# Linear attention with a gated output: units of 256 tokens in a hand-ordered order of two steps, instead of chunks of 128 tokens over all batches

## The chip, the cores and the metric

The kernel runs on one NeuronCore of a Trainium2 chip. The metric is the device time of one execution in microseconds, as the median of three runs. The engines are TensorE (PE, matmuls; PEld is its weight loading), VectorE (DVE), ScalarE (ACT), GpSimd (POOL), and SyncE (SP), which here only issues DMAs. [...] TensorE writes to PSUM[...]. All other tiles lie in SBUF.

## The reference

Batch 4, 8 heads of 48, 768 tokens; r, k, v are float32. First comes a recurrence for every batch and head, with a decay w per channel and a bonus u for the token itself:

```
for t in range(S):
    y[t]  = r[t] @ (state + (u*k[t]) outer v[t])
    state = w[:, None] * state + k[t] outer v[t]
```

The heads side by side give x, 384 wide, and a gated layer follows:

```
gate_pre[t] = sum over j < 5 of conv_w[j] * x[t - 4 + j]      # causal, per channel
out = (sigmoid(gate_pre) * (x @ w_val)) @ w_out
```

Both kernels compute the recurrence in chunks of 128 tokens. Within a chunk, r is scaled by powers of w and so is k, the scores k r are masked to the earlier tokens and multiplied with v; the state at the chunk's start adds its part; the bonus term is a scalar per token and head, times v.

## The kernel before

One loop runs over six chunks of 128 tokens; each iteration does all 4 batches and 8 heads (32 pairs of batch and head, `NPAIR` = 16 pairs of heads). The framework's scheduler sets the order of the instructions on each engine, so work of two chunks is mixed.

1. Loads: for each batch r, k and v of the chunk (lines 145 to 153), in pieces of one head's 48 numbers, that is 192 bytes.
2. VectorE scales r (L163), k (L169) and makes u*k (L175), each 128x1536, into `rkd`. GpSimd multiplies r by u*k (L182, `rku`), VectorE sums over each head (L186, `diagval`), GpSimd multiplies by v (L188, `diagv`). ScalarE casts v (L195).
3. TensorE transposes r and k in pairs of heads (L204), 8 to a PSUM tile; ScalarE copies these out (L211, `rkT`).
4. Scores: for each head a matmul over 48 rows (L226), four heads to a PSUM tile `at_ps`. VectorE masks three of four such tiles (L236); for the fourth ScalarE copies (L244) and GpSimd masks (L245).
5. y: for each head the state's part (L270; odd heads sit 64 partitions higher, so the state is kept twice, `z_lo` and `z_hi`) and the scores' part (L282), in PSUM as tokens by channels, 48 columns each. VectorE adds the bonus (L291).
6. State: k times v per head (L302), 48 wide, plus the old state through an identity (L310); VectorE applies the decay (L318); a DMA copies `z_lo` to `z_hi`.
7. Gated layer: TensorE transposes y (L331), ScalarE copies to `xT` (L336). For each third of the channels: five matmuls with diagonal matrices make the convolution (L346), ScalarE takes the sigmoid (L353), three matmuls make the value (L357), VectorE multiplies (L364). For each batch three matmuls project (L372), ScalarE copies out (L380), a DMA stores.

All of step 7's sums use one PSUM buffer, which has one copy:

```
g_ps = ps_mm.tile([128, B, 128], F32, name="mm_ps", bufs=1)
```

`at_ps0`, `at_ps1`, `y_ps_e`, `y_ps_o` and `s_ps` have one copy each too, `tp_ps` has two.

Of the kernel before, what the change touches and what calls it, by code (L numbers as in the profile page):

```python
# [16 lines left out]
def kernel(  # L18
# [16 lines left out]
    NCH = S // C  # L35
    BH = B * H
    NPAIR = BH // 2
    DM = H * D
    KW = moe_conv_w.shape[0]
    NQ = DM // 128  # L40
    SPAD = KW - 1
    TPB = SPAD + S

    consts = ctx.enter_context(tc.tile_pool(name="consts", bufs=1))
    persist = ctx.enter_context(tc.tile_pool(name="persist", bufs=1))
    statep = ctx.enter_context(tc.tile_pool(name="statep", bufs=3))
    ld = ctx.enter_context(tc.tile_pool(name="ld", bufs=2))
    wk = ctx.enter_context(tc.tile_pool(name="wk", bufs=2))
    atpool = ctx.enter_context(tc.tile_pool(name="atpool", bufs=1))
    moep = ctx.enter_context(tc.tile_pool(name="moep", bufs=2))  # L50
    outp = ctx.enter_context(tc.tile_pool(name="outp", bufs=4))

    ps_tp = ctx.enter_context(tc.tile_pool(name="ps_tp", bufs=2, space=bass.MemoryType.PSUM))
    ps_at = ctx.enter_context(tc.tile_pool(name="ps_at", bufs=1, space=bass.MemoryType.PSUM))
    ps_ys = ctx.enter_context(tc.tile_pool(name="ps_ys", bufs=1, space=bass.MemoryType.PSUM))
    ps_mm = ctx.enter_context(tc.tile_pool(name="ps_mm", bufs=1, space=bass.MemoryType.PSUM))

    ident = consts.tile([128, 128], BF16)
    make_identity(nc, ident)

    mask = consts.tile([128, 128], BF16)
    make_upper_triangular(nc, mask, val=1.0, diag=False)

    w_bc = consts.tile([128, H, D], F32)
    nc.sync.dma_start(out=w_bc, in_=w.partition_broadcast(128))
    lnw_bc = consts.tile([128, H, D], F32)
    nc.scalar.activation(out=lnw_bc, in_=w_bc, func=AF.Ln)

    io_i32 = consts.tile([128, 1], mybir.dt.int32)
    nc.gpsimd.iota(io_i32, pattern=[[0, 1]], base=0, channel_multiplier=1)  # L70
    io_f = consts.tile([128, 1], F32)
    nc.vector.tensor_copy(io_f, io_i32)
    sc_q = consts.tile([128, 1], F32)
    nc.vector.tensor_scalar_add(sc_q, io_f, float(-C))
# [3 lines left out]
    )  # L78

    dq = consts.tile([128, H, D], F32)  # L80
    nc.scalar.activation(out=dq, in_=lnw_bc, func=AF.Exp, scale=sc_q)
    dk2 = consts.tile([128, H, D], F32)
    nc.scalar.activation(out=dk2, in_=lnw_bc, func=AF.Exp, scale=sc_k)
    u_bc = consts.tile([128, H, D], F32)
    nc.sync.dma_start(out=u_bc, in_=u.partition_broadcast(128))

    wt_t = consts.tile([48, H], F32)
    nc.sync.dma_start(out=wt_t, in_=w.rearrange("h d -> d h"))
    wct = consts.tile([48, H], F32)
    nc.scalar.activation(out=wct, in_=wt_t, func=AF.Ln)  # L90
    nc.scalar.activation(out=wct, in_=wct, func=AF.Exp, scale=float(C))

    wstage = consts.tile([128, NQ, DM], F32)
    nc.sync.dma_start(out=wstage, in_=moe_w_val.rearrange("(t p) n -> p t n", p=128))
    wval = consts.tile([128, NQ, DM], BF16)
    nc.vector.tensor_copy(wval, wstage)
    wstage2 = consts.tile([128, NQ, DM], F32)
    nc.sync.dma_start(out=wstage2, in_=moe_w_out.rearrange("(t p) n -> p t n", p=128))
    wout = consts.tile([128, NQ, DM], BF16)
    nc.vector.tensor_copy(wout, wstage2)  # L100

    convw = consts.tile([128, NQ, KW], F32)
    convw_src = moe_conv_w.rearrange("t (q p) -> p q t", p=128)
    for q in range(NQ):
        nc.sync.dma_start(out=convw[:, q, :], in_=convw_src[:, q, :])
    cwdiag = consts.tile([128, NQ, KW, 128], BF16)
    for q in range(NQ):
        for t in range(KW):
            nc.gpsimd.memset(cwdiag[:, q, t, :], 0.0)
            nc.gpsimd.affine_select(  # L110
                out=cwdiag[:, q, t, :],
                in_=convw[:, q, t : t + 1].to_broadcast([128, 128]),
                compare_op=ALU.is_equal,
                fill=0.0,
                base=0,
                pattern=[[-1, 128]],
                channel_multiplier=1,
            )

    xT = []  # L120
    for q in range(NQ):
        t_ = persist.tile([128, B, TPB], BF16, name=f"xT_{q}")
        xT.append(t_)
        nc.vector.memset(t_[:, :, 0:SPAD], 0.0)

    z_lo = statep.tile([128, BH, D], BF16, name="z_lo")
    nc.vector.memset(z_lo[0:48], 0.0)
    z_hi = statep.tile([128, BH, D], BF16, name="z_hi")
    nc.vector.memset(z_hi[64:112], 0.0)

    TWID = 64
    PAIR_W = 3 * 2 * TWID
    rkd_tiles = []
    for i in range(2):
        t_ = persist.tile([128, NPAIR * PAIR_W], BF16, name=f"rkd_{i}")
        rkd_tiles.append(t_)
        tv = t_.rearrange("p (pr t pa x) -> p pr t pa x", pr=NPAIR, t=3, pa=2, x=TWID)
        nc.gpsimd.memset(tv[:, :, 0:2, :, D:TWID], 0.0)

    for c in range(NCH):  # L140
        t0 = c * C
        rk_sb = ld.tile([128, B, H, 2, D], F32, name="rk_sb")
        v_sb = ld.tile([128, B, H, D], F32, name="v_sb")
        for b in range(B):
            nc.sync.dma_start(
                out=rk_sb[:, b, :, 0, :],
                in_=r[b, :, t0 : t0 + C, :].transpose([1, 0, 2]),
            )
            nc.sync.dma_start(
                out=rk_sb[:, b, :, 1, :],  # L150
                in_=k[b, :, t0 : t0 + C, :].transpose([1, 0, 2]),
            )
            nc.sync.dma_start(
                out=v_sb[:, b, :, :],
                in_=v[b, :, t0 : t0 + C, :].transpose([1, 0, 2]),
            )

        rkd_flat = rkd_tiles[c % 2]
        rkd = rkd_flat.rearrange(
            "p (pr t pa x) -> p pr t pa x", pr=NPAIR, t=3, pa=2, x=TWID  # L160
        )

        nc.vector.tensor_tensor(  # L163
            out=rkd[:, :, 0, :, 0:D],
            in0=rk_sb[:, :, :, 0, :],
            in1=dq[:, None, :, :].to_broadcast([128, B, H, D]),
            op=ALU.mult,
        )
        nc.vector.tensor_tensor(  # L169
            out=rkd[:, :, 1, :, 0:D],  # L170
            in0=rk_sb[:, :, :, 1, :],
            in1=dk2[:, None, :, :].to_broadcast([128, B, H, D]),
            op=ALU.mult,
        )
        nc.vector.tensor_tensor(  # L175
            out=rkd[:, :, 2, :, 0:D],
            in0=rk_sb[:, :, :, 1, :],
            in1=u_bc[:, None, :, :].to_broadcast([128, B, H, D]),
            op=ALU.mult,
        )  # L180
        rku = wk.tile([128, B, H, D], BF16, name="rku")
        nc.gpsimd.tensor_tensor(  # L182
            out=rku, in0=rk_sb[:, :, :, 0, :], in1=rkd[:, :, 2, :, 0:D], op=ALU.mult
        )
        diagval = wk.tile([128, B, H, 1], F32, name="diagval")
        nc.vector.tensor_reduce(out=diagval, in_=rku, axis=AX.X, op=ALU.add)  # L186
        diagv = wk.tile([128, B, H, D], BF16, name="diagv")
        nc.gpsimd.tensor_tensor(  # L188
            out=diagv,
            in0=v_sb,  # L190
            in1=diagval.to_broadcast([128, B, H, D]),
            op=ALU.mult,
        )
# [218 lines left out]
```

## Time and profile before

| | before |
|---|---|
| time, median of 3 | 175.4 us (173.97 to 175.93) |
| span of the profiled run | 172.6 us |
| first matmul | 22.79 us |
| DVE busy | 102.3 us |
| ACT busy | 75.0 us |
| POOL busy | 63.6 us |
| mean granted TensorE clock | 0.888 |
| DMA | 21.54 MB in 82190 packets, 77792 of them under 512 bytes |

The span runs from the first to the last instruction of one profiled execution; the time of an unprofiled run stands a little above it. A page's "busy" is the time in which an engine had an instruction in work. For TensorE it says less, because matmuls are pipelined and overlap; the distance from one start to the next says what a matmul costs in a stream. The granted clock is the share of full speed that the throttle let TensorE have. A group row reads: line, engine, operation, output from inputs, shapes, count, then busy time in us, mean ns of one, and the idle time before it with what ended it. A window row reads: stretch, its length, then busy time and count of PE, PEld, DVE, ACT and POOL, the granted clock, the DMA share and GB/s.

### The profile page before, as it was taken

To read this page: it belongs to the slowest core of one execution; us is meant where nothing else is said; L and a number is where in the kernel's file an instruction comes from. 1 tells how busy PE (TensorE), PEld (TensorE's weight loads), DVE (VectorE), ACT (ScalarE), POOL (GpSimd) and SP (SyncE) were. 2 spreads that over 40 slices of the span, in tenths; PEclk is the share of its full clock that TensorE was granted. 3 is DMA by queue.
4 is the path that set the end of the run, shared out by engine and by line. 5 is a ranking of instruction groups with operands and counts; after the bars stand their busy time and mean duration, and the time that the engine had idled before them with its cause. 6 is when DMAs were issued, how large, how long until landed. Compare 5 with 4: busy or idle time off the path is not lost. (4 is left out here: it accounts for less than half of the span.)

```text
span 172.6 us, 3173 instructions
## 1 busy us (share of the span) xinstructions
PE 123.5 (72%) x1272; PEld 71.1 (41%) x1272; DVE 102.3 (59%) x136; ACT 75.0 (43%) x110; POOL 63.6 (37%) x65
## 2 busy tenths in 40 slices
PE   0000049668988999977998887999869998986542
PEld 0000037445544555633665444555435654542120
DVE  3120195858777848667895786864779576641200
ACT  3420047113972354942668244555373553451131
POOL 3079007830257431673015825166270653200000
PEclk9999999655799855999999998589996999999995
DMA  3999999921997178990597978938431100311022
GB/s 90 276 175 184 191 184 187 192 31 30 206 163 141 47 192 174 208 150 1 150 214 140 187 155 218 166 66 158 87 137 49 32 2 4 137 49 34 0 91 91
DMA packets 82190, 21.54 MB, mean 125 GB/s; under 512 B 77792, under 2 KB 81888, under 8 KB 82176
## 3 DMA queue, kind: packets, MB, share of 16 engines
q1 hardware_dynamic: 82176, 21.35, 66.6%
q8 instruction: 10, 0.16, 0.4%
q14 instruction: 4, 0.03, 0.1%
HBM read 15.74 MB, written 4.72 MB: 119 GB/s over the span
## 5 line engine op out<-in xcount | busy, mean ns | idle before, releaser
L204 PE MATMUL tp_ps<-ident,rkd 128*128 128x128 bf16 x192 | 16.7, 239 | 25.2 <-DVE rkd L163 22.8
L182 POOL TENSOR_TENSOR rku<-rk_sb,rkd 128x1536 bf16<-128x1536 f32 x6 | 18.5, 3090 | 42.8 <-DVE rkd L175 42.8
L236 DVE TENSOR_TENSOR at_sb<-at_ps,mask 128x512 bf16<-128x512 f32 x36 | 23.8, 685 | 9.2 <-PE at_ps L226 9.2
L346 PE MATMUL mm_ps<-xT,cwdiag 128*128 128x512 bf16 x90 | 26.7, 431 | 2.1 <-DVE hT L364 2.1
L245 POOL TENSOR_TENSOR at_sb<-at_stage,mask 128x512 bf16<-128x512 bf16 x12 | 19.5, 1621 | 22.9 <-ACT at_stage L244 22.9
L204 PEld LDWEIGHTS <-rkd 128*128 128x128 bf16 x192 | 14.2, 108 | 30.5 <-issue 26.0
L211 ACT COPY rkT<-tp_ps 128x1024 bf16<-128x1024 bf16 x24 | 23.2, 1015 | 6.1 <-PE tp_ps L204 5.9
L364 DVE TENSOR_TENSOR hT<-gp,mm_ps 128x512 bf16<-128x512 bf16 x18 | 12.3, 685 | 17.0 <-PE mm_ps L357 12.5
L380 ACT COPY out_sb<-mm_ps 128x384 f32<-128x384 f32 x24 | 11.5, 479 | 23.3 <-PE mm_ps L372 15.6
L188 POOL TENSOR_TENSOR diagv<-v_sb,diagval 128x1536 bf16<-128x1536 f32 x6 | 16.6, 2768 | 12.2 <-DVE diagval L186 12.2
L353 ACT ACTIVATE gp<-mm_ps 128x512 bf16<-128x512 f32 x18 | 10.8, 597 | 23.5 <-PE mm_ps L346 20.3
L372 PE MATMUL mm_ps<-wout,hT 128*128 128x384 bf16 x72 | 17.3, 352 | 4.2 <-ACT out_sb L380 3.3
L318 DVE TENSOR_TENSOR z_lo<-s_ps,wct 48x384 bf16<-48x384 f32 x24 | 13.1, 545 | 6.9 <-PE s_ps L310 6.9
L226 PE MATMUL at_ps<-rkT 48*128 48x128 bf16 x192 | 15.6, 229 | 1.9 <-DVE at_sb L236 1.6
L163 DVE TENSOR_TENSOR rkd<-rk_sb,dq 128x1536 bf16<-128x1536 f32 x6 | 10.5, 1758 | 10.6 <-DMA rk_sb<-in_r_dram 10.6
L357 PE MATMUL mm_ps<-xT,wval 128*128 128x512 bf16 x54 | 14.7, 380 | 2.9 <-ACT gp L353 2.4
L336 ACT COPY xT<-tp_ps 128x512 bf16<-128x512 bf16 x18 | 10.0, 589 | 13.7 <-PE tp_ps L331 13.6
L195 ACT CAST vbf<-v_sb 128x1536 bf16<-128x1536 f32 x6 | 8.8, 1474 | 11.5 <-DMA v_sb<-in_v_dram 11.5
L346 PEld LDWEIGHTS <-cwdiag 128*128 128x128 bf16 x90 | 8.9, 108 | 11.9 <-issue 6.4
L282 PE MATMUL y_ps_o<-vbf,at_sb 128*128 128x48 bf16 x96 | 8.7, 193 | 6.8 <-POOL at_sb L245 6.7
L226 PEld LDWEIGHTS <-rkT 48*128 48x128 bf16 x192 | 8.7, 98 | 11.5 <-issue 10.3
L186 DVE TENSOR_REDUCE diagval<-rku 128x32 f32<-128x1536 bf16 x6 | 10.5, 1752 | 4.4 <-POOL rku L182 4.3
(46 smaller groups left out, 153.2 us busy)
## 6 DMA issues: line engine op xcount, KB each, us to landing
rk_sb<-in_r_dram SPq DMA_DIRECT2D x24, 192.0 KB, 4.7
rk_sb<-in_k_dram SPq DMA_DIRECT2D x24, 192.0 KB, 4.5
v_sb<-in_v_dram SPq DMA_DIRECT2D x24, 192.0 KB, 4.6
out_dram<-out_sb SPq DMA_DIRECT2D x24, 192.0 KB, 1.9
z_hi<-z_lo SPq DMA_DIRECT2D x6, 144.0 KB, 2.7
wstage<-in_moe_w_val_dram SPq DMA_DIRECT2D x1, 576.0 KB, 5.2
wstage<-in_moe_w_out_dram SPq DMA_DIRECT2D x1, 576.0 KB, 6.5
w_bc<-in_w_dram SPq DMA_DIRECT2D x1, 192.0 KB, 3.3
```

Source lines behind the costliest of these rows:

```text
L182: nc.gpsimd.tensor_tensor(out=rku, in0=rk_sb[:, :, :, 0, :], in1=rkd[:, :, 2, :, 0:D], op=ALU.mult)
L188: nc.gpsimd.tensor_tensor(out=diagv, in0=v_sb, in1=diagval.to_broadcast([128, B, H, D]), op=ALU.mult,)
L204: nc.tensor.transpose(tp_ps[:, 2 * pp + t, :], rkd_flat[:, pair * PAIR_W + t * 128 : pair * PAIR_W + (t + 1) * 128], ident,)
L211: nc.scalar.copy(out=rkT[:, g * n_tp_grp : (g + 1) * n_tp_grp, :, :], in_=tp_ps)
L226: nc.tensor.matmul(out=at_ps[:, q, :], lhsT=rkT[pbase : pbase + 48, pair, 1, :], rhs=rkT[pbase : pbase + 48, pair, 0, :], start=(q == 0), ...
L236: nc.vector.tensor_tensor(out=dst, in0=at_ps, in1=mask[:, None, :].to_broadcast([128, n_at_grp, 128]), op=ALU.mult,)
L245: nc.gpsimd.tensor_tensor(out=dst, in0=stage, in1=mask[:, None, :].to_broadcast([128, n_at_grp, 128]), op=ALU.mult,)
L318: nc.vector.tensor_tensor(out=z_lo_new[0:48, b * H : (b + 1) * H, :], in0=s_ps[0:48], in1=wct[:, :, None].to_broadcast([48, H, D]), op=ALU ...
L346: nc.tensor.matmul(out=g_ps, lhsT=cwdiag[:, q, t, :], rhs=xT[q][:, :, SPAD + t0 - shift : SPAD + t0 + C - shift], start=(t == 0), stop=(t ...
L357: nc.tensor.matmul(out=val_ps, lhsT=wval[:, kt, q * 128 : (q + 1) * 128], rhs=xT[kt][:, :, SPAD + t0 : SPAD + t0 + C], start=(kt == 0), st ...
L364: nc.vector.tensor_tensor(out=hT[:, q], in0=gp[:, q], in1=val_ps, op=ALU.mult)
L372: nc.tensor.matmul(out=o_ps, lhsT=hT[:, q, b, :], rhs=wout[:, q, :], start=(q == 0), stop=(q == NQ - 1),)
```

## The change

The whole kernel body is rewritten; inputs, outputs and the chunked form of the recurrence stay.

- Work is cut into 12 units: one batch, 256 tokens, that is two chunks of 128. The order on each engine is now written out by hand (`manual_schedule`): iteration i does the front part of unit i (scores, bonus scalars, state) and the back part of unit i-1 (y, convolution, value, projection), and prepares unit i+1 (casts, scaling, transposes).
- r is loaded for a whole batch in runs of 6 tokens of one head (1152 bytes) and transposed once per batch; the copy out of PSUM puts the tokens in order. Its scaling runs on GpSimd in iterations 1 to 7, ahead of the bonus product (`bonus_v`) in the same iteration.
- k's scaling moves from VectorE to GpSimd.
- The bonus: VectorE multiplies the transposed k by the transposed r once (`prod`), and small matmuls of two columns against u*w sum it per head (`bonus`).
- States are kept for a pair of heads on all 128 partitions, with zeros off the diagonal blocks (`wcm`), so the second copy and its DMA go.
- y is made with the channels on the partitions, in groups of 32 channels: the weights are 32 columns of z, v or the bonus, the moving operand is r, the scores or the identity. So the transposes of y go.
- The convolution's first two thirds of the channels use 64x64 diagonal blocks.
- The sums use one pool of three PSUM buffers (`mm_ps`); the scores use one tile of two banks per chunk.
- TensorE is kept busy at the start by 130 matmuls without use (`spin`).

The purpose is to keep TensorE fed with work whose inputs are already there, to shorten the start, and to move elementwise work off VectorE.

The diff, cut to its core (helpers of the setup and casts left out):

```
-    for c in range(NCH):
-        t0 = c * C
...
+    ctx.enter_context(tc.manual_schedule())
...
+    def load_r(b):
+        r_st[b] = ldr.tile([128, H, J * D], F32, name="r_st")
+        nd = NP if b == 0 else 2
+        for hh in range(nd):
+            hs = slice(hh * (H // nd), (hh + 1) * (H // nd))
+            nc.sync.dma_start(
+                out=r_st[b][:, hs, :],
+                in_=r[b, hs].rearrange("h (p j) d -> p h (j d)", j=J),
+            )
...
+    load_r(0)
+    load_kv(0, "kv")
+    load_kv(1, "k")
...
+    def prod(n):
+        st["pr", n] = wk.tile([128, NP, W], BF16, name="pr")
+        nc.vector.tensor_tensor(
+            out=st["pr", n].rearrange("x n (c i) -> x c n i", c=U),
+            in0=st["tr", n],
+            in1=rTu(n).rearrange("x n (c i) -> x c n i", c=U),
+            op=ALU.mult,
+        )
+    def bonus(n):
+        s_ps = ps_mm.tile([128, U, H], F32, name="mm_ps")
+        pr = st["pr", n]
+        for cl in range(U):
+            for p in range(NP):
+                nc.tensor.matmul(
+                    out=s_ps[:, cl, 2 * p : 2 * p + 2],
+                    lhsT=pr[:, p, cl * C : cl * C + C],
+                    rhs=uw2[:, p, :],
+                    start=(cl == 0 and p == 0),
+                    stop=(cl == U - 1 and p == NP - 1),
+                    skip_group_check=True,
+                )
+        st["s", n] = wk.tile([128, U, H], F32, name="s_sb")
+        nc.vector.tensor_copy(st["s", n], s_ps)
...
+    def attn(n, cl):
+        rT, kT = rTu(n), st["kT", n]
+        cs = slice(cl * C, cl * C + C)
+        at_ps = ps_at.tile([128, 2, NP, 128], F32, name="at_ps")
+        for p in range(NP):
+            for par in range(2):
+                rows = slice(64 * par, 64 * par + D)
+                nc.tensor.matmul(
+                    out=at_ps[:, par, p, :],
+                    lhsT=kT[rows, p, cs],
+                    rhs=rT[rows, p, cs],
+                    start=(p == 0),
+                    stop=(p == NP - 1),
+                    skip_group_check=True,
+                )
...
+    def state(n, cl):
+        c = (n % NU) * U + cl
+        if c == NU * U - 1:
+            return
+        ks, vb = ks_t[n % 3], vb_t[n % 4]
+        kv_ps = ps_kv.tile([128, NP, 2, D], F32, name="kv_ps")
+        for p in range(NP):
+            nc.tensor.matmul(
+                out=kv_ps[:, p],
+                lhsT=ks[:, cl, p].rearrange("p a x -> p (a x)"),
+                rhs=heads(vb[:, cl], H)[:, 2 * p : 2 * p + 2, :],
+                start=(p == 0),
+                stop=(c == 0 and p == NP - 1),
+                skip_group_check=True,
+            )
+        if c > 0:
+            nc.tensor.matmul(
+                out=kv_ps.rearrange("p n a d -> p (n a d)"),
+                lhsT=ident,
+                rhs=st["z"].rearrange("p n a d -> p (n a d)"),
+                start=False,
+                stop=True,
+                skip_group_check=True,
+            )
+        st["kv_ps", n, cl] = kv_ps
...
+            z = st.get(("zin", n, cl))
+            if z is not None:
+                zf = z.rearrange("p n a d -> p (n a d)")
+                for G in range(3 * NP):
+                    mm(G, zf[:, 32 * G : 32 * G + 32], rT[:, G // 3, cl * C : cl * C + C])
+            at = st["at", n, cl]
+            for x in range(2):
+                for h in range(H):
+                    p, par = divmod(h, 2)
+                    c0 = ((16, 32), (48, 0))[x][par]
+                    mm(
+                        3 * p + (1 if x else 2 * par),
+                        vb[:, cl, 64 * h + c0 : 64 * h + c0 + 32],
+                        at[:, par, p, :],
+                    )
+            for G in range(3 * NP):
+                mm(G, dv[:, cl, 32 * G : 32 * G + 32], ident, last=True)
+            t0 = PAD + cu * W + cl * C
+            nc.scalar.copy(out=xT_t[b % 2][:, :, t0 : t0 + C], in_=y_ps)
...
+        g1 = ps_mm.tile([128, W], F32, name="mm_ps")
+        g02 = ps_mm.tile([128, 2, W], F32, name="mm_ps")
+        for t in range(KW):
+            for q in range(2):
+                for T in range(2):
+                    rows = slice(64 * q, 64 * q + 64)
+                    qo = (q + T) % 2
+                    g = g1 if T else g02[:, 0, :]
+                    nc.tensor.matmul(
+                        out=g[64 * qo : 64 * qo + 64],
+                        lhsT=cwd[rows, T, t, :],
+                        rhs=xT[rows, T, t0 + t : t0 + t + W],
+                        start=(t == 0),
+                        stop=(t == KW - 1),
+                        skip_group_check=True,
+                    )
...
+    load_weights()
+    load_kv(1, "v")
+    load_kv(2, "k")
+    spin(130)
+    scale_r(0, 0, nc.vector)
+    scale_r(0, 1, nc.vector)
+    scale_r(0, 2, nc.vector)
+    scale_k(0, nc.vector)
+    scale_r(0, 3, nc.vector)
+    transp_r(0, 0)
+    transp_r(0, 1)
+    transp_k(0)
+    transp_r(0, 2)
+    transp_r(0, 3, dve=True)
+    prod(0)
+    cast_v(0)
+    nc.scalar.preload_act_table_set("sigmoid_and_others")
...
+    r_plan = {
+        1: (1, (0, 1), (0, 1)),
+        2: (1, (2, 3), (2, 3)),
+        3: (2, (0, 1), (0, 1)),
+        4: (2, (2, 3), (2, 3)),
+        5: (3, (0,), ()),
+        6: (3, (1, 2), (0, 1)),
+        7: (3, (3,), (2, 3)),
+    }
+    r_load = {0: 1, 2: 2, 4: 3}
+    for i in range(N + 1):
+        f = i - 1
+        if i == 0:
+            load_kv(2, "v")
+        if i in r_load:
+            load_r(r_load[i])
+        if ok(i + 3):
+            load_kv(i + 3, "kv")
+        rb, sp, tp = r_plan.get(i, (0, (), ()))
+        if ok(f):
+            y_out(f)
+        if ok(i + 1):
+            cast_v(i + 1)
+            scale_k(i + 1, nc.gpsimd)
+        if ok(i):
+            attn(i, 0)
+            mask_at(i, 0)
+            bonus(i)
+            state(i, 0)
+            decay(i, 0)
+        for p in sp:
+            scale_r(rb, p, nc.gpsimd)
+        if ok(i):
+            bonus_v(i)
+        if i == 0:
+            prep_diag()
+            cast_weights()
+        if ok(f):
+            conv(f)
+            value(f)
+        if tp:
+            transp_r(rb, tp[0])
+        if ok(i):
+            attn(i, 1)
+            mask_at(i, 1)
+            state(i, 1)
+            decay(i, 1)
+        if tp:
+            transp_r(rb, tp[1])
+        if ok(i + 1):
+            transp_k(i + 1)
+            prod(i + 1)
+        if ok(f):
+            project(f)
+# ---- launch: one core; inputs and outputs as the reference has them ----
+_INS = ['r', 'k', 'v', 'w', 'u', 'moe_w_val', 'moe_conv_w', 'moe_w_out']
+_OUTS = [((4, 768, 384), 'float32')]
```

## The prediction

> **What bounds the kernel now.** I read four views in this order: the page's engine shares and slices, the chain of waits, the timeline of TensorE (PE) by shape, and windows for the granted clock.
>
> ```profile
> PE 123.5 (72%) x1272; PEld 71.1 (41%) x1272; DVE 102.3 (59%) x136; ACT 75.0 (43%) x110; POOL 63.6 (37%) x65
> PE   0000049668988999977998887999869998986542
> PEclk9999999655799855999999998589996999999995
> DMA  3999999921997178990597978938431100311022
> GB/s 90 276 175 184 191 184 187 192 31 30 206 163 141 47 192 174 208 150 1 150 214 140 187 155 218 166 66 158 87 137 49 32 2 4 137 49 34 0 91 91
> ```
>
> PE is empty for five slices (4.3 us each) while DMA is full, then never idle long. So there is a start of 22.8 us and a loop of 150 us. "Busy" overstates PE because matmuls overlap, so I price PE by start-to-start time. This is the timeline of PE: start, length, line, shape, count.
>
> ```profile
> 49.32 0.61 PE L204 MATMUL tp_ps<-ident,rkd 128*128 128x128 bf16 x8
> 50.16 0.81 PE L357 MATMUL mm_ps<-xT,wval 128*128 128x512 bf16 x3
> 50.90 0.23 PE L226 MATMUL at_ps<-rkT 48*128 48x128 bf16 x1
> 53.55 0.41 PE L226 MATMUL at_ps<-rkT 48*128 48x128 bf16 x8
> 45.74 0.38 PE L302 MATMUL s_ps<-vbf,rkd 128*48 128x48 bf16 x8
> ```
>
> One L357 alone lasts 380 ns (page row), so three in 0.81 us start (0.81-0.38)/2 = 215 ns apart: 0.42 ns a column, hence 54 ns for 128 columns, 108 for 256, 162 for 384. L204 agrees (about 55 ns). Eight L226 with K=48 in alternating row halves start (0.41-0.22)/7 = 27 ns apart: two run side by side. L302, 48 columns wide, needs about 28 ns. The L226 at 50.90 follows the third L357 (started 50.59) by 0.31 us instead of 0.215: a change of tile shape costs 95 ns.
>
> At these prices the old PE work is 144x0.215 + 96x0.162 + 264x0.054 + 192x0.04 + 576x0.027 = 84 us, plus some 180 shape changes (counted in the order of the trace) of 0.095 = 17 us: 101 us.
>
> ```profile
> 40.00:44.00 4.00, 3.54 (x21) 1.90 (x19) 3.56 (x4) 2.56 (x4) 0.00 (x0) 0.50 0.35 71
> 64.00:68.00 4.00, 4.00 (x27) 2.30 (x27) 3.87 (x4) 1.66 (x3) 0.00 (x0) 0.50 0.87 189
> 72.00:76.00 4.00, 3.72 (x49) 2.16 (x48) 3.59 (x5) 2.47 (x4) 1.52 (x1) 1.00 1.42 195
> ```
>
> The windows' PEclk column (third from the end) is 0.50 in two of these three. Mean clock over 28 to 168 us is 0.88, so a quarter of it ran at half speed: about 17 us lost. 101 + 17 = 118 of 150 us. The other 30 us are round trips; the chain shows how:
>
> ```profile
> 160.73 1.27 PE mm_ps L346 x5
> 162.02 0.61 ACT gp L353
> 162.67 0.82 PE mm_ps L357 x3
> 163.59 0.70 DVE hT L364
> ```
>
> One PSUM buffer (mm_ps, one deep) carries convolution, value and projection, so PE waits for each reader. In the loop other work fills some of it; from 152 us on nothing does.
>
> [...] No 32-column tile is in this trace. [...] The trace has the halving, but in windows where PE is busy, so I can't say when it will strike. [...] the same masking takes 1.15 us, and 3.07 beside L163:
>
> ```profile
> 98.42 1.15 POOL L245 TENSOR_TENSOR at_sb<-at_stage,mask 128x512 bf16<-128x512 bf16 x1 [0.57 <-ACT at_stage L244]
> 102.91 3.07 POOL L245 TENSOR_TENSOR at_sb<-at_stage,mask 128x512 bf16<-128x512 bf16 x1 [3.34 <-ACT at_stage L244]
> ```
>
> After the change no DVE instruction of the loop has two SBUF inputs, so I take GpSimd at its free rates.
>
> **PE after, over the whole run** (12 units).
> - y_out: 912 matmuls, 32 columns of weights by 128 moving (20 chunks of 40, 4 of 28). Consecutive ones go to different column groups, except the second score pass, which comes in pairs on one group. Fully parallel is 54/4 = 13.5 ns, not at all 54. I take 22: the two row tiles here halve exactly[...]. 20.1 us (12 to 49).
> - Convolution: 240 matmuls in four 64x64 tiles, 27 ns if four run together, 108 if none; I take 33: 7.9 us (6.5 to 26). 60 full ones x 0.108 = 6.5. It replaces 90x0.215 = 19.4.
> - Value 108x0.108 = 11.7; projection 72x0.162 = 11.7 (as before).
> - Transposes 192x0.054 = 10.4; the 72 of y go, since y_out writes y already transposed. Scores 192x0.028 = 5.4.
> - Bonus 96 two-column matmuls at 25 ns (floor of the short ones here): 2.4. State 80x0.041 + 16x0.162 = 5.9; the copy of the state to the upper partitions by DMA goes.
> - Shape changes, 7 a unit: 84x0.095 = 8.0.
>
> Sum 90 us (80 to 140), of which 3.6 fall before the second iteration (40 transposes, unit 0's scores, bonus, state): 86 remain, some 7.5 us an iteration.
>
> **The other engines per unit**, from these rows:
>
> ```profile
> L236 DVE TENSOR_TENSOR at_sb<-at_ps,mask 128x512 bf16<-128x512 f32 x36 | 23.8, 685 | 9.2 <-PE at_ps L226 9.2
> L211 ACT COPY rkT<-tp_ps 128x1024 bf16<-128x1024 bf16 x24 | 23.2, 1015 | 6.1 <-PE tp_ps L204 5.9
> ```
>
> DVE: 685 ns for 512 is 150 + 1.04 an element. Two masks of 1024 (2.4), product with the transposed k (1024 from PSUM[...]: 1.2), two gate products (1.1), 1.7 decays (0.9), a copy (0.15): 5.8 us. ACT: k copy 1.0, 1.25 r copies of 0.8, v cast 0.8, y copies 2x0.48, sigmoids 0.4+0.6, output copies 2x0.48: 5.7. GpSimd: 3.09 us for 1536 elements (page) is 2.0 ns each[...] bonus product 768x1.8 = 1.4: 4.4 to 5.7. All lie below PE's 7.5 and beside it. What is queued behind their waits: attn of the second chunk waits for the first mask (one at_ps), but convolution and value stand between; the k copy waits behind two r copies, but projection and y_out stand between. I leave 0.4 us an iteration exposed: 11x0.4 = 4.4.
>
> **DMA.** 192-byte rows run at about 186 GB/s (slices 2 to 7), 1536-byte rows at 276 (slice 1). k and v 9.4 MB: 51 us; r, now in 1152-byte runs, output and weights 10.8 MB: 39 us. 90 us in all, beside PE, five buffers deep: hidden except at the start.
>
> **Start.** Now PE's first work waits for chunk 0 of r, which lies behind all weights:
>
> ```profile
> 20.89 1.76 DVE L163 TENSOR_TENSOR rkd<-rk_sb,dq 128x1536 bf16<-128x1536 f32 x1 [10.57 <-DMA rk_sb<-in_r_dram]
> 22.79 0.37 PE L204 MATMUL tp_ps<-ident,rkd 128*128 128x128 bf16 x2 [22.79 <-DVE rkd L163]
> ```
>
> After, unit 1's v comes behind w, r of batch 0, k and v of unit 0, k of unit 1 and the weights: 1.57 MB at 186 + 1.97 MB at 276 = 15.6 us, from about 2: 17.6. ACT then casts it, converts w_out (1.1) and copies k (1.0): 20.5, while y_out of unit 0 can start at 18. I take 19.5. The other path gives less: w lands at 4.1 (L67 now), the decay tables (0.5, twelve of 0.4, one of 0.6) take ACT to 10.0, three scalings (2.5), transposes, a copy and the product (2.2) to 14.7. GpSimd's bonus product ends near 17, the diagonals[...] and weight casts[...] near 23, when convolution first needs them.
>
> **Sum.** 19.5 + 86.4 + 4.4 = 110.3; last unit's unshared waits 1.5, last output copy and store 2.4: 114; clock loss 4 (half speed for 8 us[...]): 118. The measured time stands 175.4-172.6 = 2.8 above the span: **121 us**.
>
> **Rivals.**
> - The 32-column tiles don't run side by side: 49 instead of 20 us, so 150. For: all use the same rows. Against: L302 hides its weight loads and row tiles overlap. Chance 0.12.
> - The fixed order exposes hand-overs: mask 1.2 and k copy 1.0 unhidden in each of 11 iterations, +24: 145. For: at_ps and kv_ps are one deep. Against: the order puts 2 us of matmuls between. 0.17.
> - Slower: short column-tiled matmuls keep the clock at half through the loop: 121 + 82 = 203. For: half clock strikes busy windows now. Against: only a quarter of the time. 0.05.
> - The forecast, 0.66. Its lower end: no clock loss, y_out at 13.5 ns: 121-4-8 = 109; a little less wait, 107.
>
> The range 107 to 148 takes in the forecast, most of the hand-over case and part of the column case. Faster 0.94, within 1% 0.01, slower 0.05.
>
> **What would show it.** PE's y_out starts some 22 ns apart; the 64x64 tiles about 33; an iteration of 7.5 us with PE the engine that waits least; y_out of unit 0 near 19 us; mean clock above 0.9; GpSimd's k scale at 1.7. Wrong if y_out starts 50 ns apart, if PE waits over 1 us an iteration for a copy or mask, or if the first loads land past 25 us.

## The result, and the profile after

| | before | after |
|---|---|---|
| time, median of 4 | 174.69 us (172.62 to 175.93) | 117.19 us (116.48 to 117.86) |
| span of the profiled run | 172.6 us | 115.8 us |
| mean granted TensorE clock | 0.888 | 0.937 |
| DVE, ACT, POOL busy | 102.3, 75.0, 63.6 us | 67.7, 73.0, 66.3 us |

The ratio is 0.6752 (95% interval 0.6688 to 0.6817): faster by a third. It is no quotient of the medians, because executions of one kernel come in a faster and a slower state, and it compares only the runs of the faster one. The forecast was 121 us. First the page, the engine shares and three of its rows of slices (2.9 us each).

```profile
PE 100.0 (86%) x2098; PEld 76.5 (66%) x2098; DVE 67.7 (58%) x120; ACT 73.0 (63%) x130; POOL 66.3 (57%) x62
...
PE   5999046889899999999979999999999999998840
...
PEclk9999975555999999999999999999999999999998
GB/s 44 240 270 150 95 236 305 194 193 266 277 191 180 292 332 169 256 213 253 341 170 248 154 248 113 256 206 96 238 169 147 0 133 8 24 118 6 136 3 136
```

The half clock is now one stretch in the start, from 15.8 to 29.5 us, and PE is full from there to the end. One warning on this row and on the mean clock: where a profile has no clock record yet, they count full clock. Here the records begin at 5.6 us (in the kernel before at 28.1), and ahead of that the matmuls without use start 107 ns apart, after it 56: TensorE began at half speed. Cutting the span where y_out of unit 0, y_out of unit 1 and y_out of the last unit start gives this table (columns: length, busy time and count of PE, PEld, DVE, ACT, POOL, then clock, DMA share, GB/s):

```profile
0.00:22.90 22.90, 15.39 (x203) 13.91 (x203) 11.31 (x34) 12.47 (x24) 11.40 (x24) 0.85 0.90 192
22.90:34.10 11.20, 10.22 (x164) 7.06 (x162) 5.49 (x9) 6.98 (x11) 10.98 (x11) 0.71 1.03 235
34.10:105.70 71.60, 69.48 (x1617) 52.02 (x1617) 49.65 (x76) 50.13 (x90) 43.95 (x29) 1.00 0.72 178
105.70:115.80 10.10, 4.93 (x121) 3.47 (x120) 1.27 (x3) 3.46 (x8) 0.00 (x0) 0.95 0.23 80
```

There are three regimes. Up to 34 us the DMA share is 0.90 and 1.03, and GpSimd is busy for 10.98 of the 11.20 us of the second stretch; the experiments below ask which of the two holds the start. From 34.1 to 105.7 us ten iterations take 7.16 us each; the clock is 1.00 and PE is busy 97% of the time, and these are all its waits in that stretch (engine, tile, line, releaser: total us, times, longest):

```profile
PE mm_ps L435 <- issue: 0.9, 1, 0.9
PE mm_ps L383 <- ACT o_sb L482: 0.5, 2, 0.3
PE mm_ps L475 <- DVE hT L463: 0.3, 1, 0.3
```

That is 1.7 us in ten iterations. The loop is bound by the matmuls themselves. One iteration of the chain of waits (start, length, what) prices them:

```profile
41.78 1.30 PE mm_ps L383 x80
...
43.89 0.67 PE mm_ps L426 x20
44.56 0.66 PE mm_ps L435 x5
```

The 80 y_out matmuls take 1.30 us: 16.3 ns each, against 54 ns for the same 128 columns at full width. In the records four of them start within 10 to 20 ns, then the next four 55 ns later. The 64x64 tiles are at 0.67/20 = 34 ns.

Two rows of the page give prices of the other engines:

```profile
L245 POOL TENSOR_TENSOR ks<-k_st,dk 128x768 bf16<-128x768 f32 x11 | 20.0, 1815 | 5.5 <-DMA k_st<-in_k_dram 5.5
L279 DVE TENSOR_TENSOR pr<-tr_ps,rT 128x1024 bf16<-128x1024 bf16 x12 | 8.3, 692 | 7.9 <-ACT kT L268 7.6
```

The k scale costs about what was forecast (1.7 us), and so does the mask (1220 ns for 1.2). The product L279 costs 0.69, not 1.2.

### The profile page after: what moved, and what is told of

The parts are those of the page before. It is cut to its first block, busy times and chain, and to the rows that moved or that the text cites. A ratio compares the mean times of both kernels' runs of the same rounds, so it can differ in the third digit from the quotient of the medians.

```text
span 115.8 us, 4806 instructions
## 1 busy us (share of the span) xinstructions
PE 100.0 (86%) x2098; PEld 76.5 (66%) x2098; DVE 67.7 (58%) x120; ACT 73.0 (63%) x130; POOL 66.3 (57%) x62
## 4 chain that ended last, share of the span: by engine, by line
PE 55%; ACT 10%; SPq 10%; POOL 10%; issue 6%; DMA 4%; DVE 1%; POOLq 0%; ACTq 0%; DVEq 0%
PE mm_ps L383 9%; PE mm_ps L456 9%; SPq L72 8%; PE mm_ps L426 6%; PE mm_ps L435 6%; PE mm_ps L475 6%; PE at_ps L317 5%; ACT kT L268 4%; DMA k_st<-in_k_dram 4%; PE tr_ps L238 3%; PE kv_ps L343 3%; POOL ks L245 3%; ACT o_sb L482 3%; ACT rT L239 3%; PE mm_ps L291 2%
## 5 line engine op out<-in xcount | busy, mean ns | idle before, releaser
L329 DVE TENSOR_TENSOR at<-at_ps,mask 128x1024 bf16<-128x1024 f32 x24 | 29.3, 1220 | 8.8 <-PE at_ps L317 8.8
L303 POOL TENSOR_TENSOR dv<-v_st,s_sb 128x768 bf16<-128x768 f32 x12 | 17.7, 1475 | 24.3 <-DVE s_sb L300 24.3
L245 POOL TENSOR_TENSOR ks<-k_st,dk 128x768 bf16<-128x768 f32 x11 | 20.0, 1815 | 5.5 <-DMA k_st<-in_k_dram 5.5
L463 DVE TENSOR_TENSOR hT<-mm_ps,gate 128x256 bf16<-128x256 f32 (+1 forms) x24 | 13.4, 558 | 15.3 <-PE mm_ps L456 15.3
L226 POOL TENSOR_TENSOR rs<-r_st,dr 128x576 bf16<-128x576 f32 x12 | 16.7, 1412 | 3.2 <-DMA r_st<-in_r_dram 3.1
L268 ACT COPY kT<-tr_ps 128x1024 bf16<-128x1024 bf16 x12 | 12.2, 1014 | 8.6 <-PE tr_ps L265 8.6
L239 ACT COPY rT<-tr_ps 128x768 bf16<-128x768 bf16 x15 | 11.9, 799 | 7.0 <-PE tr_ps L238 7.0
L456 PE MATMUL mm_ps<-xT,wval 128*128 128x256 bf16 x108 | 13.8, 272 | 0.0
L279 DVE TENSOR_TENSOR pr<-tr_ps,rT 128x1024 bf16<-128x1024 bf16 x12 | 8.3, 692 | 7.9 <-ACT kT L268 7.6
L411 ACT CAST xT<-mm_ps 128x384 bf16<-128x384 f32 x24 | 11.8, 496 | 1.0 <-PE mm_ps L383 0.2
L368 DVE TENSOR_TENSOR z<-kv_ps,wcm 128x384 bf16<-128x384 f32 x20 | 11.0, 548 | 0.0
L444 ACT ACTIVATE gate<-mm_ps 128x512 bf16<-128x512 f32 x12 | 7.2, 597 | 4.6 <-PE mm_ps L435 4.6
```

Of the source, the lines that this page charges most:

```text
L226: eng.tensor_tensor(out=rs_t[p][:, :, :, 0:D].rearrange("p j a d -> p a j d"), in0=r_st[b][:, hs, :].rearrange("p a (j d) -> p a j d", d=D ...
L239: (nc.vector.tensor_copy if dve else nc.scalar.copy)(out=st["rT", b][:, p, :].rearrange("x (p j) -> x p j", j=J), in_=tr.rearrange("x j p ...
L245: eng.tensor_tensor(out=ks_t[n % 3][:, :, :, :, 0:D].rearrange("p c n a d -> p c (n a) d"), in0=k_st[n], in1=dk[:, None, :, :].to_broadcas ...
L268: nc.scalar.copy(out=st["kT", n].rearrange("x n (c i) -> x c n i", c=U), in_=tr)
L303: nc.gpsimd.tensor_tensor(out=dv_t[n % 2].rearrange("p c (h d) -> p (c h) d", d=D), in0=v_st[n].rearrange("p c h d -> p (c h) d"), in1=st[ ...
L329: nc.vector.tensor_tensor(out=st["at", n, cl].rearrange("p a n i -> p (a n) i"), in0=st["at_ps", n, cl].rearrange("p a n i -> p (a n) i"), ...
```

## The experiments

Twelve kernels ran, each the changed kernel with one edit (e10 has several, e11 none). The kernel before ran beside each, at 175.0 to 175.8 us; "ratio" is to it. The changed kernel itself, run again as e11, gave 117.32.

### Do the column tiles run side by side? (e1)

The 40 matmuls of a chunk are issued column group by column group, ten in a row on one, instead of in turn on four.

```diff
             def mm(G, lt, rh, last=False):
+                todo.append((G, lt, rh, last))
+
+            def issue(G, lt, rh, last):
                 T, q = divmod(G, 4)
...
+            for one in sorted(todo, key=lambda x: x[0] % 4):
+                issue(*one)
```

> The same 912 matmuls of y in another order: all of one 32-column group (10 in a row), then the next group. Forecast's step (column groups run side by side, 40 in 0.74 us after the change, 18 ns each): they now take 128 columns' time each, 54 ns, so y goes from 16 to 49 us and the kernel from 117 to about 148 us, with TensorE still the engine that waits least. Rival (short matmuls are limited by the issue of instructions, not by their place in the array): still about 18 ns each, kernel within 2 us of 117.

Measured: 133.40 us, ratio 0.7707 (0.7631 to 0.7782), 16 us slower than the changed kernel. First its chain, then its timeline of PE (start, length, line, shape, count):

```profile
61.24 3.12 PE mm_ps L386 x80
```

```profile
61.34 0.39 PE L386 MATMUL mm_ps<-at,vb 128*32 128x128 bf16 x4
61.52 0.23 PE L386 MATMUL mm_ps<-rT,z 128*32 128x128 bf16 x1
61.57 0.22 PE L386 MATMUL mm_ps<-ident,dv 128*32 128x128 bf16 x1
61.58 0.22 PE L386 MATMUL mm_ps<-rT,z 128*32 128x128 bf16 x1
```

Four in a row on one group start (0.39-0.22)/3 = 57 ns apart: no parallelism within a group. So the gain of the changed kernel comes from parallelism between groups. But the 80 take 3.12 us, 39 ns each, not 54. The lines show why: the last three of one group (dv) are issued before the first three of the next (z), yet their starts alternate (and so on for two more of each). Three of ten run beside the neighbour group, so a group takes about 7 x 55 ns. An iteration is 8.58 us against 7.16; the iterations in the start, which wait for loads, hide the rest. The mechanism stands, at half the size that I expected.

### What do the 64x64 tiles give? (e4)

The 20 tiles of the convolution's first two thirds become 10 full-width diagonal matmuls, and the swap of halves goes.

```diff
-            for q in range(2):
-                for T in range(2):
...
-                        lhsT=cwd[rows, T, t, :],
-                        rhs=xT[rows, T, t0 + t : t0 + t + W],
...
+            for T in range(2):
+                nc.tensor.matmul(
+                    out=g1 if T else g02[:, 0, :],
+                    lhsT=cwd[:, T, t, :],
+                    rhs=xT[:, T, t0 + t : t0 + t + W],
```

> The convolution's first two thirds with full 128x128 diagonal matrices (10 matmuls of 256 columns) instead of 20 in 64x64 tiles; the order of the channels in the gate, the value and the projection is set to fit. Prediction's price: 10 x 0.108 = 1.08 us against 0.67 us for the 20 tiles, which includes one change of shape: +0.4 us a unit, kernel 4 to 5 us slower. Rival (the tiles save nothing, because the change of shape and 20 weight loads eat it): within 1 us.

Measured: 119.87 us, ratio 0.6930 (0.6857 to 0.7003), 2.7 us slower. Its chain:

```profile
44.34 1.10 PE mm_ps L420 x10
45.44 0.55 PE mm_ps L429 x5
```

The ten take 1.10 us, against 0.67 for the twenty tiles. The five full ones behind them take 0.55 instead of 0.66: without the tiles there is no change of shape ahead of them, and the 110 ns are close to the 95 of the forecast. Net 0.32 us a unit, 3.8 over twelve, of which 2.6 reach the span. The tiles help, but they are a small part.

### Do hand-overs between engines matter? (e2, e3, e7)

e2 gives the PSUM ring `mm_ps` two buffers instead of three:

```diff
-    ps_mm = ctx.enter_context(tc.tile_pool(name="ps_mm", bufs=3, space=bass.MemoryType.PSUM))
+    ps_mm = ctx.enter_context(tc.tile_pool(name="ps_mm", bufs=2, space=bass.MemoryType.PSUM))
```

> The ring of PSUM buffers for the sums has two instead of three. Theory (the loop gains because hand-overs are covered by the three buffers and the order): each iteration TensorE now waits for the bonus copy before the convolution (0.7 us), for the second sigmoid before the second value tile (0.5), for the output copies before y (0.8 and 0.4): about 2.3 us an iteration, kernel about 117 + 25 = 142 us. Rival (TensorE work alone sets the time, the third buffer is spare): within 3 us of 117.

Measured: 136.21 us, ratio 0.7859 (0.7762 to 0.7957), 19 us slower. PE's two longest waits over the whole run:

```profile
PE mm_ps L383 <- ACT o_sb L482: 6.6, 10, 0.8
PE mm_ps L426 <- DVE s_sb L300: 6.1, 11, 0.7
```

With 3.9 us for the gate (L444) ahead of the value matmuls they sum to 16.6 us. They come in nearly every unit, at the three places where the next sum needs the buffer that a copy, a gate or the bonus is still reading. With three buffers the first costs 0.5 us from 34 us on, and the others don't appear. So the hand-over rival describes a kernel one buffer away from this one.

e3 puts the bonus product ahead of the r scaling in GpSimd's queue:

```diff
-        for p in sp:
-            scale_r(rb, p, nc.gpsimd)
         if ok(i):
             bonus_v(i)
+        for p in sp:
+            scale_r(rb, p, nc.gpsimd)
```

> On GpSimd the bonus product comes before the scaling of r instead of behind it. Theory: GpSimd then stands waiting for the bonus scalars (24 us of such waits in the profile after), and r's pieces come 1.5 to 2 us late for their transposes in iterations 1 to 4 and 6: kernel 5 to 9 us slower, TensorE waiting at the transposes of r for GpSimd. Rival (GpSimd has slack, 57% busy): within 1 us of 117.

Measured: 124.34 us, ratio 0.7169 (0.7081 to 0.7258), 7.1 us slower. Two of its waits:

```profile
POOL dv L303 <- DVE s_sb L300: 33.9, 11, 5.3
PE tr_ps L238 <- POOL rs L226: 5.5, 6, 1.5
```

In the changed kernel the first reads `24.3, 9, 5.3`. The bonus product needs the sums that TensorE makes early in the same iteration. When it stands first, GpSimd idles 9.6 us more, the r scaling behind it starts late, and TensorE waits 5.5 us for it. Part of the difference may be chance: the profile of e3 has a second stretch of half clock, 3.4 us long from 51.6 us, which can have cost 1.7 us at most. So r scaled ahead of the bonus rows is worth 5 to 7 us.

e7 moves the k scaling to VectorE:

```diff
-            scale_k(i + 1, nc.gpsimd)
+            scale_k(i + 1, nc.vector)
```

> k of units 1 to 11 is scaled by VectorE (0.96 us each, two SBUF inputs) instead of GpSimd (1.8). Theory: TensorE sets the pace of the loop and waits for neither engine, so the loop stays as it is and the kernel is within 2 us of 117. Rival (VectorE is close to the bound, 67.7 us busy now[...]): 11 x 0.96 us added, part of it on the path, 4 to 10 us slower.

Measured: 117.32 us, ratio 0.6771 (0.6607 to 0.6935): no difference.

```profile
L245 DVE TENSOR_TENSOR ks<-k_st,dk 128x768 bf16<-128x768 f32 x12 | 14.4, 1200 | 1.0 <-DMA k_st<-in_k_dram 1.0
```

VectorE's busy time rises to 79.4 us and GpSimd's falls to 46.9, and neither is seen in the time. In these two runs the order within a queue counts, not the load of an engine that TensorE outlasts.

### What bounds the start? (e5, e6, e8, e9, e10, e11, e12)

y_out of unit 1 starts at 34.1 us, 11.2 after that of unit 0. Candidates are the half clock, GpSimd's list of diagonals and casts, and the loads. The chain of waits of the changed kernel seems to blame GpSimd, whose bonus product, diagonals (L198, L206), weight casts, k and r scalings follow each other on it from 20.9 to 32.2 us:

```profile
22.38 1.22 POOL cwd L198
...
27.60 1.75 POOL ks L245
...
30.80 1.42 POOL rs L226
```

e5 takes away the 130 matmuls that keep TensorE busy while loads come:

```diff
     load_kv(2, "k")
-    spin(130)
     scale_r(0, 0, nc.vector)
```

> The 130 matmuls without use at the start are left out. Theory: they end at 10.8 us, long before the loads let TensorE work steadily; the clock falls to half at 15 us in spite of them, so the kernel is within 1 us of 117. Rival (they keep the first iterations at full clock): half clock from the first transposes on, 3 us or more slower.

Measured: 117.07 us, ratio 0.6787 (0.6622 to 0.6952). The same stretch, from y_out of unit 0 to y_out of unit 1:

```profile
22.00:33.10 11.10, 8.25 (x163) 5.85 (x162) 5.39 (x9) 6.74 (x11) 10.95 (x11) 1.00 1.02 238
```

At full clock PE has 8.25 us of work there instead of 10.22, and the stretch is as long as before: the clock alone wasn't the bound. GpSimd is busy for 10.95 of the 11.10 us. TensorE waits 1.5 us for its r scaling, which began at 28.43, after the list ahead of it, though r of batch 1 had landed at 27.98.

The clock of 1.00 holds only for this stretch. The clock records of e5 begin at 22.9 us; ahead of that its eight transposes of k take 1.03 us, against 0.62 in the changed kernel (first e5, then the changed kernel):

```profile
13.27 1.03 PE L265 MATMUL tr_ps<-ident,ks 128*128 128x128 bf16 x8 [2.99 <-DVE ks L245]
14.60 0.62 PE L265 MATMUL tr_ps<-ident,ks 128*128 128x128 bf16 x8 [3.14 <-DVE ks L245]
```

That is 107 ns from start to start instead of 56. The eight at 21.03 us in e5 still take 1.06 us, those at 31.59 us 0.61. So without the 130 matmuls TensorE ran at half speed at 13.27 and at 21.03 us, with them from 15.8 to 29.5: the half speed moves, and the time stays the same.

e6 makes the diagonals before the loop:

```diff
+    prep_diag()
+
     r_plan = {
...
         if i == 0:
-            prep_diag()
             cast_weights()
```

> GpSimd makes the convolution's diagonals (3.8 us) ahead of the loop, while it waits for k of unit 1, instead of behind the first bonus product. The chain of waits of the changed kernel puts these 3.7 us on the path that sets the end: if the chain is right, 3 to 4 us faster, 113. Theory: the second iteration waits for loads as well (v of unit 2 lands at 27.7 us, r of batch 1 at 29.3 and 31.0), so the gain is at most 1 us.

Measured: 118.17 us, ratio 0.6849 (0.6719 to 0.6978); y_out of unit 1 at 34.3. No gain: GpSimd now stands where it worked (first the changed kernel, then e6):

```profile
29.44 2.76 POOL L226 TENSOR_TENSOR rs<-r_st,dr 128x576 bf16<-128x576 f32 x2
29.61 2.77 POOL L226 TENSOR_TENSOR rs<-r_st,dr 128x576 bf16<-128x576 f32 x2 [2.96 <-PE mm_ps L435]
```

It waits 2.96 us ahead of the first piece of r of batch 1. The view names PE for this wait, but r landed at 29.48, 0.13 us ahead of the start, as in the changed kernel (29.31 and 29.44), where GpSimd came from its list at 29.38 and had nothing to wait for. So the chain's GpSimd pieces weren't time that could be taken out alone: r landed just as GpSimd got to it. The edit has a price of its own too: the diagonals now run beside VectorE's scaling of k of unit 0, which took 1.93 us instead of 0.96, which may be why y_out of unit 0 came only 0.2 us earlier (22.79) although that k landed 1.1 us earlier.

e8 issues the small loads of w, u and conv_w from ScalarE's queue, to test whether GpSimd's own transfers slow the big ones:

```diff
-            nc.gpsimd.dma_start(
+            nc.scalar.dma_start(
...
```

> The seven loads of single numbers (w, u, conv_w) are issued by ScalarE instead of GpSimd. Theory: k and v of unit 0 and 1 landed late (10.9 to 17.4 us) because the transfers beside GpSimd's ran at 70 to 160 GB/s between 8 and 14 us; without it they land 2 to 3 us earlier and so do all loads behind them: kernel 2 to 3 us faster. Rival (192-byte rows are that slow at the start whoever issues the small ones): within 1 us of 117.

Measured: 119.65 us, ratio 0.6910 (0.6783 to 0.7037). k of unit 1 landed at 17.05 us (17.4 before), so the hoped-for 2 to 3 us didn't come. The test isn't clean, though: k of unit 0 was issued 4.0 us later (7.20 for 3.18) and still landed 1.0 us earlier (12.48 for 13.49), and VectorE's first r scaling, which waits for ScalarE's decay tables, began at 10.62 instead of 7.95. In the profiled run 0.4 us of the rise were there at y_out of unit 0; another 1.3 came by unit 1, where half clock struck a second time (32.9 to 36.3 us) and the projection took 2.13 us instead of 1.14. The interval still touches that of the changed kernel.

e9 transposes all of batch 1's r in the third iteration, so that the second needs none of it, and in the second puts the bonus product ahead of the r scaling:

```diff
-        1: (1, (0, 1), (0, 1)),
-        2: (1, (2, 3), (2, 3)),
+        1: (1, (0, 1), ()),
+        2: (1, (2, 3), (0, 1, 2, 3)),
...
```

> r of batch 1 is transposed in the third iteration instead of half in the second, half in the third; in the second GpSimd makes the bonus product first. Theory (the second iteration ends late because it waits for r of batch 1, which lands at 29.3 and 31.0 us): y of unit 1 starts 1 us earlier than the 34.1 us it has now, the third iteration gets 0.7 us of transposes more, kernel 0.3 to 1 us faster, since half clock still holds the second iteration. Rival (TensorE's own work at half clock alone sets it): y of unit 1 earlier by the 0.7 us moved and no more, kernel unchanged.

Measured: 117.53 us, ratio 0.6744 (0.6690 to 0.6797). y_out of unit 1 started 2.8 us earlier (31.30), but that of unit 2 at 41.3 instead of 41.7. Its timeline in the third iteration:

```profile
35.20 0.83 ACT L254 CAST vb<-v_st 128x768 bf16<-128x768 f32 x1 [2.00 <-DMA v_st<-in_v_dram]
36.37 0.82 PE L456 MATMUL mm_ps<-xT,wval 128*128 128x256 bf16 x6 [1.07 <-ACT gate L443]
```

ScalarE stood 2.0 us for v of unit 3, so the gates behind that cast came late and PE waited 1.07 us for them; then four copies of r stood in a row on ScalarE (2.9 us from 37.55), ahead of the copy of k. The 2.8 us were given back at the next load.

e10 puts the start's ideas together: e5, e6, e9, and w_out loaded behind v of unit 2 (its cast one iteration later).

```diff
             load_kv(2, "v")
+            load_wout()
...
+        if i == 1:
+            nc.scalar.copy(out=wout, in_=wo_st)
```

> The late r, the diagonals made early, no matmuls without use, and w_out loaded behind v of unit 2 (cast in the second iteration). Theory (the start is bound by the loads, in the order in which they are issued): v of unit 1 lands 2 us earlier, y of unit 0 starts near 20.5 and y of unit 1 near 31 us; the third iteration gets 0.7 us more; kernel 2 to 3 us faster, 114 to 115. Rival (GpSimd's and ScalarE's work between the loads sets the start): 1 us or less.

Measured: 116.73 us, ratio 0.6691 (0.6631 to 0.6751). y_out started at 23.1, 31.1 and 40.7 us for units 0, 1 and 2: 1.0 us gained by unit 2 (the two stretches took 8.0 and 9.6 us, against 11.2 and 7.6). For the comparison e11, the changed kernel without an edit, ran beside it:

> The changed kernel itself once more, on the chip of these runs, as the measure for the two others: 117 us.

Measured: 117.32 us, ratio 0.6728 (0.6656 to 0.6799). The 0.6 us between e10 and e11 lie within these intervals. No version here is shown to beat the changed kernel.

e12 goes at the transfers themselves: k and v in runs of 384 bytes, one DMA a unit. The two chunks of a unit then hold every second token each, so this kernel leaves out the order of the tokens.

```diff
-            for cl in range(U):
-                t0 = cu * W + cl * C
-                nc.sync.dma_start(
-                    out=d[n][:, cl], in_=src[b, :, t0 : t0 + C, :].transpose([1, 0, 2])
-                )
+            nc.sync.dma_start(
+                out=t_,
+                in_=src[b, :, cu * W : cu * W + W, :].rearrange("h (p c) d -> p h (c d)", c=U),
+            )
```

> k and v are loaded in runs of two tokens of one head (384 bytes) by one DMA a unit, instead of 192 bytes by two; the two chunks of a unit then hold every second token, so this kernel doesn't compute the reference's order of tokens. All work on the engines is the same. Theory (until unit 3's v has landed, at 34 us, the loads bound the kernel, at 15 to 16 ns a 192-byte row and engine): the 3.1 MB of k and v until then take about a third less, the loads end some 5 us earlier, and the kernel is 3 to 5 us faster, 112 to 114 us. Rival (the engines' work bounds the start, late loads only fill it): within 1 us of 117.

Measured: 115.55 us, ratio 0.6652 (0.6538 to 0.6766); the span is 113.4, 2.4 less. VectorE's scaling of k of unit 0, first in the changed kernel, then in e12:

```profile
13.58 0.96 DVE L245 TENSOR_TENSOR ks<-k_st,dk 128x768 bf16<-128x768 f32 x1 [2.30 <-DMA k_st<-in_k_dram]
11.38 0.96 DVE L245 TENSOR_TENSOR ks<-k_st,dk 128x768 bf16<-128x768 f32 x1
```

k of unit 0 landed 2.1 us earlier (11.36 for 13.49), the wait of 2.30 us is gone, and y_out of unit 0 came 2.1 us earlier (20.9), that of unit 1 as well (32.0). So the first part of the start, up to y_out of unit 0, hangs on the load of k. The second part does not on loads alone: r of batch 1 landed 2.7 us earlier (26.61), and the stretch from y_out of unit 0 to that of unit 1 stayed at 11.1 us.

```profile
20.90:32.00 11.10, 9.81 (x167) 7.07 (x170) 5.32 (x9) 7.42 (x11) 10.95 (x11) 0.69 1.08 269
27.28 2.76 POOL L226 TENSOR_TENSOR rs<-r_st,dr 128x576 bf16<-128x576 f32 x2
```

GpSimd was busy for 10.95 us of it, as in e5, and reached r 0.7 us after it had landed; TensorE, at half clock until 27.8 us, didn't wait for it. So in the changed kernel three things end together in the second part: GpSimd's list (29.38), the landing of r (29.31) and TensorE's work at half clock, which waits only 0.4 us for the first scaled piece. e5 takes away the half clock, and TensorE waits for GpSimd's list; e6 shortens the list, and GpSimd waits for r; e12 brings r early, and the other two remain. A kernel with none of the three was not run.

The gain stayed below what I expected. One reason may be that second part; another is that a 384-byte packet took 27.2 ns in the mean against 16.3 for 192 bytes (medians 22 and 15). The ratio's interval overlaps that of the changed kernel, so the gain in time is likely, not shown.

## Why the prediction was right, and where it was off

By its own steps, in span:

| step | forecast, us | measured, us | difference |
|---|---|---|---|
| y_out of unit 0 starts | 19.5 | 22.95 | +3.4 |
| PE work from there | 86.4 | 81.2 | -5.2 |
| clock loss; measured: the first iteration's excess, 11.2 - 7.2 | 4 | 4.0 | 0 |
| waits in the loop | 4.4 | 1.7 | -2.7 |
| last unit and output, beside PE's work | 3.9 | 5.2 | +1.3 |
| not accounted for | | 0.8 | +0.8 |
| span | 118.2 | 115.8 | -2.4 |

The 81.2 is not measured but worked out: the forecast's sum with y_out at 912 x 16.3 ns = 14.9 instead of 20.1 us; the tail is 10.10 us with 4.93 of PE work in it. Time over span was 1.4, not 2.8 us.

- **Bound.** Right. I named PE as the loop's bound after the change, and it waits 1.7 us in 71.6. An iteration of 7.16 us lies near the 7.5 named.
- **y_out.** The mechanism was right, and e1 shows it. The term was mis-sized, 22 for 16.3 ns: the 22 was my estimate, with no column tile in the trace before to measure it by, while four column tiles came to 55/16.3 = 3.4. In e1 the starts alternate between two groups (z at 61.52, 61.58 and 61.64 us, dv at 61.57, 61.62 and 61.68), so by these records each column group goes on with its own.
- **64x64 tiles, value, projection, shape changes.** Right: 34 for 33 ns, 0.98 us for nine value and 0.97 us for six projection matmuls against 0.97 each, and about 110 for 95 ns a change (e4).
- **Hand-overs.** Right that the order covers them, but what I named for it was the matmuls between. e2 shows that the third buffer of `mm_ps` is needed too, which the forecast didn't name: without it 19 us come back.
- **GpSimd.** k 1815, r 1412 and bonus 1475 ns against 1.7, 1.3 and 1.4 us: right. The first two were my estimates, above the 2.0 ns an element of L182 in the kernel before; k and r took 2.4 (1815/768 and 1412/576). What the forecast left out is that the order of its queue is worth 5 to 7 us (e3).
- **The product with the transposed k.** Wrong, without effect on the time. I put it at 1.2 us, which is also where 1024 elements lie between the 685 ns for 512 (L236) and 1758 for 1536 (L163) of the kernel before. With all operands bf16 1024 elements took 692 ns (L279), while the mask from f32 PSUM took 1220 (L329).
- **Start.** This step failed, in the loads and in GpSimd's list. "1.57 MB at 186 + 1.97 MB at 276" put v of unit 1 at 17.6 us; it landed at 22.5. The 1.97 MB have only one of the two weight matrices, and both were loaded ahead of that v: with 2.56 MB the same rates give 19.7, so 2.1 of the 4.9 us are this sum and 2.8 the rates. The path that set y_out of unit 0 was the one that I put at 14.7 us, because I left out when k lands. By the same rates k of unit 0 would land near 9 us; it landed at 13.5, and the chain from it (scaling, transposes, scores, the second mask until 22.67) runs up to y_out of unit 0 at 22.95 (e12). The GB/s row shows 150 and 95 in the slices from 8.7 to 14.5 us: the DMA engines were first busy at a low rate, then (12 to 14 us) had a share of only 0.32 while a single issue on the load queue lasted from 10.0 to 13.05 us. The second part: I had GpSimd's bonus product end near 17 us and its diagonals and casts near 23; they ended at 22.4 and 27.6, and with the k and r scalings behind them this list is one of the three things that held y_out of unit 1. I had the loads hidden "except at the start", and the start lasted until 34 us.
- **Clock.** Half speed did come, from about 16 to 29 us, but beside GpSimd's list and the loads, where taking it away alone gave nothing (e5). My 4 us stood for a loss that was there, from other causes. That is luck, not insight.

Where the 57 us of span came from, with the forecast's estimates for before: PE work 101 to 81.2, about 20; the throttled clock 17 to nothing that taking it away gave back (e5), about 17; waits and tail 30 to 11.7 (1.7, 5.2, 0.8 and the first iteration's excess of 4.0), about 18. These are estimates and leave 2 us over. The start stayed as it was (22.8, 22.95). e1 and e4 stand for the first, e2 and e3 for the third. Why the clock falls in the loop before and not in the loop after was not settled.

Also open: why the transfers were slow from 8.7 us on, and why single issues on the load queue took 3.1 us there. The gap from 12 to 14 us (share 0.32) isn't in every kernel: without the 130 matmuls the share there is 1.01 (e5) and 0.88 (e10), with the small loads on ScalarE 0.93 (e8), with long rows 1.19 (e12). No run tells what these have in common. And no run takes the kernel before and makes one of the changes there, so what the fixed order, the missing transposes and the new form of the state give, each for itself, isn't shown.

## What to carry to other kernels

Sum TensorE by start-to-start prices per shape, and issue narrow column tiles so that neighbours fall in different column groups: that alone was 16 us here. Here the fixed order hid the hand-overs only with a third PSUM buffer for the sums still being read, and without it 19 us came back (e2); take one away and look at the waits. A chain of waits names the last releaser, not what can be saved: before shortening a piece of it, ask which load lands just behind, and before speeding up a load, which engine's list ends just behind that. Check a clock row against the distance of matmul starts: here it said 1.00 where they stood 107 ns apart, not 56.

## What the runs showed of the hardware

- Four 32-column tiles of 128 moving columns: 16.3 ns a matmul (80 in 1.30 us, changed kernel) against 57 in a row within one group (e1). By the start times on record, matmuls of the next column group started ahead of earlier ones in the program: z at 61.52 us, the dv issued before it at 61.57 (e1).
- Half speed in the start came with and without the 130 matmuls: from 15.8 to 29.5 us in the changed kernel, at 13.27 and 21.03 us in e5 (eight transposes of k in 1.03 and 1.06 us, 0.61 at 31.59). The clock row shows 1.00 for the latter two, since the clock records begin only at 22.9 us; the 107 ns between the starts tell. The stretches of half clock in the clock records, apart from those in the last microseconds of a run, lasted 13.65, 10.24, 6.83 and 3.41 us in the kernel before (from 31.5, 58.8, 106.6 and 130.5 us) and 13.65 in the changed kernel: one, two, three or four times 3.41.
- VectorE's scaling of k, with two SBUF inputs, took 0.96 us alone (changed kernel) and 1.93 beside GpSimd's diagonals (e6); the first two of these took 3.19 us instead of 2.58. In the kernel before, the three of GpSimd's twelve maskings (L245) that ran beside VectorE's L163 took 2.94 to 3.08 us, the nine others 1.15 to 1.16.
- Twice the bytes in a piece in HBM took 1.5 to 1.7 times the time of a packet: 22 ns for 15 in the median, 27.2 for 16.3 in the mean (384 against 192 bytes, e12 and the changed kernel).
